# Storing the tail chunk of an attention-and-FFN kernel in halves of 64 rows

## The chip, the core and the metric

The kernel runs on one core of a Trainium2 chip. The metric is the device time of one execution in microseconds (us); lower is better. A core has five engines with a queue of their own each: TensorE (PE, with its weight loads PEld), VectorE (DVE), ScalarE (ACT), GpSimd (POOL) and SyncE (SP). In this kernel SP does no arithmetic: it issues DMA transfers and waits on semaphores.

## The reference

The inputs q, k and v have the shape 8 batches x 8 heads x 576 positions x 64. An attention without a score matrix is followed by a gated feed-forward network without a nonlinearity:

```
q_s = softmax(q, over the 64 features)
k_s = softmax(k, over the 576 positions)
kv  = einsum('bhsd,bhse->bhde', k_s, v)
x   = einsum('bhsd,bhde->bhse', q_s, kv)      -> 4608 tokens x 512
out = ((x @ w1) * (x @ w2)) @ w3 @ w_out      (w1, w2: 512 x 1024; w3: 1024 x 1024; w_out: 1024 x 512)
```

The output is 4608 x 512 in float32.

## The kernel before

Everything is multiplied in float16 and summed in float32. The product of w3 and w_out is made once at the start (`W3O`), so that a chunk needs two products of the first kind (`up`, with w1 and w2), one elementwise product (`ab`) and one product of the second kind (`down`, with `W3O`).

A batch has 576 tokens, nine for each of 64 rows (`HALF` = 64, `NJ` = 9: token = 9 * row + j). The main chunks, c = 0 to 7, take j = 0 to 7 of batch c, 512 tokens. What is left, j = 8 (`NM`) of all eight batches, is collected in `xtail` and makes a ninth chunk of 512 tokens, c = 8: the tail chunk. It runs last. Each chunk's second product goes over four blocks of 128 tokens (`tb` = 0 to 3) into the PSUM tile `po`; ACT or DVE copies a block to the SBUF tile `osb` (four buffers), and SP stores it.

- In a main chunk (`down`, `os`, `store`, the last at L824 to L829) a block holds two values of j, 64 rows each, so it is stored by two DMAs of 64 rows by 512 columns. Their rows lie nine rows of the output apart.
- In the tail chunk (`down2`, `os2`, `tail`, the last at L808 to L811) a block's 128 rows also lie nine rows of the output apart, and one DMA stores all of them. The fourth block is computed, copied and stored in two pieces of 256 columns (`c0`, `c1`), so there are five pieces: blocks 0, 1 and 2 whole, and then block 3's left and right part. In the names of the steps they are `8.0`, `8.1`, `8.2`, `8.3.0` and `8.3`.

The order of all steps on all engines is written out by hand in `ORDER`; a step is emitted where it stands there, and `PICKS` says which engine copies. The end of it is

```
down.8.0 os.7.3 st.7.3 down.8.1 os.8.0 st.8.0 down.8.2 os.8.1
st.8.1 down.8.3.0 os.8.2 st.8.2 down.8.3 os.8.3.0 st.8.3.0 os.8.3 st.8.3
```

where `st` is a store, so SP issues each store after the copy that it needs and before the next. The copies of blocks 0, 1, 2 and of the right part of block 3 are ACT's, that of the left part is DVE's.

Semaphores are given by the framework. The DMAs that SP issues take eight semaphores (0 to 7) in turn, and a DMA waits until the last one on the same semaphore has landed. When all is issued, SP waits for what is outstanding and closes the program (L915): nine wait instructions, the first for older semaphores of POOL's DMAs alone, the next eight for SP's DMA semaphores 0 to 7 in that order, most of them with another semaphore beside; then a drain, a barrier over all engines, and the clearing of the semaphores.

Of the kernel before, what the change touches and what calls it, by code (L numbers as in the profile page):

```python
# [229 lines left out]
def kernel(  # L230
# [11 lines left out]
    nc = tc.nc  # L242
    B, H, S, D = q.shape
    T, C = out.shape
    Fd = moe_w1.shape[1]
    P = 128
# [4 lines left out]
    HALF = P // G  # L251
    HH = H // G
    NHP = HH // 2
    NJ = S // HALF
    NM = 512 // HALF
# [32 lines left out]
    st = {}  # L288
# [476 lines left out]
    def chunk(c):  # L765
# [40 lines left out]
            copy(eng, st["osb", c, tb], st["po", c, tb])  # L806

        def tail(tb, c0, c1):  # L808
            nc.sync.dma_start(
                out=out.rearrange("(r j) c -> r j c", j=NJ)[tb * P:(tb + 1) * P, NM, c0:c1],  # L810
                in_=st["osb", c, tb, c0])  # L811

        def down2(tb, c0, c1):
            st["po", c, tb, c0] = p_o()
# [5 lines left out]
        def os2(tb, c0, c1, eng):  # L820
            st["osb", c, tb, c0] = work.tile([P, c1 - c0], F32, tag="osb", name="osb", bufs=4)
            copy(eng, st["osb", c, tb, c0], st["po", c, tb, c0][:, 0:c1 - c0])
# [29 lines left out]
        for sub in range(nf):  # L852
            for tb in range(4):
                if not SUBS[c][sub][0] <= tb * P < SUBS[c][sub][1]:
                    continue
                first = tb * P == SUBS[c][sub][0]
                needs = (([("ab", c, sub, u) for u in range(nu - 1)] + [("W3O", ft) for ft in range(N_FT)]
                          if first else []) + ([("down", c, tb - 1)] if tb else []))
                late = [("ab", c, sub, nu - 1)] if first else []
                if c < B:  # L860
                    A(("down", c, tb), "PE", 1.75, lambda tb=tb: down(tb), needs, takes="po", after=late)
                    A(("os", c, tb), moves(C), 0, lambda eng, tb=tb: os(tb, eng), [("down", c, tb)],
                      lead=EVICT, gives=[("down", c, tb)], takes="osb")
                    A(("st", c, tb), "SP", 1.15, lambda tb=tb: store(tb), [("os", c, tb)], lead=1e3,
                      gives=[("os", c, tb)], size=P * C * 4)
                    continue
                cuts = [0, C // 2, C] if tb == 3 else [0, C]
                for c0, c1 in zip(cuts, cuts[1:]):
                    it = (c, tb, c0) if c1 < C else (c, tb)
                    A(("down", *it), "PE", 0.02 + 1.73 * (c1 - c0) / C,  # L870
                      lambda tb=tb, c0=c0, c1=c1: down2(tb, c0, c1), needs, takes="po", after=late)
                    A(("os", *it), moves(c1 - c0), 0,
                      lambda eng, tb=tb, c0=c0, c1=c1: os2(tb, c0, c1, eng), [("down", *it)],
                      lead=EVICT, gives=[("down", *it)], takes="osb")
                    A(("st", *it), "SP", 0.57, lambda tb=tb, c0=c0, c1=c1: tail(tb, c0, c1),
                      [("os", *it)], lead=1e3, gives=[("os", *it)], size=P * (c1 - c0) * 4)
                    needs, late = needs + [("down", *it)], []
# [42 lines left out]
```

## Time and profile before

| | |
|---|---|
| median of three runs | 240.99 us (240.94 to 241.41) |
| the profiled execution | 240.52 us |
| its span, first to last instruction | 238.4 us |
| granted TensorE clock | 1.000 |
| PE busy | 230.7 us, 97% of the span |
| DVE, ACT, POOL busy | 180.0, 120.7 and 112.8 us |
| DMA | 45.66 MB, 192 GB/s on the mean |
| stores of the main chunks (L827) | 64, each 128 KB |
| stores of the tail chunk (L809) | 3 of 256 KB, 2 of 128 KB |

The span counts from the first to the last instruction; the profiled execution's own time has 2.1 us more around it. All times in the views are from the start of the span. A line of the timeline shows the start, the duration, the engine, the line of the kernel and the operation; "SPq" is SP's queue, and the duration of a DMA there is how long SP is busy issuing it, not how long the data take. The time from the start of the issue until the semaphore has its full count is called landing. In the views of one line, three numbers with slashes are the least, the median and the greatest duration in ns.

### The profile page before, as it was taken

What the parts mean: (1) busy time and instruction counts of PE and PEld (TensorE: products, weight loads), DVE (VectorE), ACT (ScalarE), POOL (GpSimd) and SP (SyncE); (2) the same over time, 40 slices, a digit from 0 to 9 for tenths busy, and PEclk for the clock granted to TensorE, in tenths of its full rate; (3) what the DMA queues carried; (4) which work ended last, traced back from release to release, by engine and by line L of the source; (5) the groups of instructions that cost most, each with busy time, mean ns of one, the idle gap of its engine ahead of it and who ended that gap; (6) DMA issues with size and microseconds to landing.
All of it is one profiled execution on the core that took longest, in us unless ns stands there. A gap on an engine that the chain in (4) does not pass through costs nothing.

```text
span 238.4 us, 4957 instructions
## 1 busy us (share of the span) xinstructions
PE 230.7 (97%) x1981; PEld 121.1 (51%) x1981; DVE 180.0 (76%) x275; ACT 120.7 (51%) x221; POOL 112.8 (47%) x74
## 2 busy tenths in 40 slices
PE   7899899999999999999999999999999999999994
PEld 2445559865857544444444444444454444444442
DVE  2977998898899989998998899787567444355610
ACT  1436764668768958768824683557323002200021
POOL 8345445479957986997662933328530000000000
PEclk9999999999999999999999999999999999999999
DMA  6999999999989999688988932540077231030143
GB/s 209 215 294 223 322 220 301 261 370 392 389 210 291 403 205 294 243 235 203 327 270 200 306 147 46 77 111 0 0 150 173 62 71 45 0 91 0 44 132 132
DMA packets 37894, 45.66 MB, mean 192 GB/s; under 512 B 15984, under 2 KB 22384, under 8 KB 37872
## 3 DMA queue, kind: packets, MB, share of 16 engines
q1 hardware_dynamic: 30080, 34.22, 49.3%
q0 software_dynamic: 7792, 11.14, 21.3%
q8 instruction: 15, 0.25, 0.4%
q14 instruction: 7, 0.06, 0.1%
HBM read 38.80 MB, written 9.44 MB: 202 GB/s over the span
## 4 chain that ended last, share of the span: by engine, by line
PE 86%; DMA 5%; DVE 3%; POOL 2%; issue 1%; ACT 1%; POOLq 0%; ACTq 0%
PE pab L779 52%; PE po L801 23%; DMA wosb<-in_moe_w_out_dram 5%; PE po L816 3%; PE pkv L544 2%; PE po L452 2%; PE xm L662 1%; DVE k L519 1%; POOL en L614 1%; POOL w L402 1%; PE po L662 1%; DVE kmx L493 1%; ACT ek L527 0%; PE pkv L554 0%; PE qtp L629 0%
## 5 line engine op out<-in xcount | busy, mean ns | idle before, releaser
L779 PE MATMUL pab<-x,w2sb 128*128 128x512 f16 (+1 forms) x320 | 66.0, 337 | 0.1
L779 PE MATMUL pab<-x,w1sb 128*128 128x512 f16 (+1 forms) x320 | 65.9, 336 | 0.0
L794 DVE TENSOR_TENSOR ab<-pab,bsb 128x512 f16<-128x512 f32 x72 | 48.9, 681 | 16.7 <-PE pab L779 15.2
L801 PE MATMUL po<-W3O,ab 128*128 128x512 f16 x256 | 59.5, 379 | 0.0
L779 PEld LDWEIGHTS <-w1sb 128*128 128x128 f16 x352 | 34.4, 98 | 27.9
L779 PEld LDWEIGHTS <-w2sb 128*128 128x128 f16 x352 | 33.4, 98 | 27.0 <-issue 0.7
L323 ACT CAST bsb<-pab 128x512 f16<-128x512 f32 x49 | 28.3, 585 | 36.5 <-PE pab L779 36.2
L801 PEld LDWEIGHTS <-ab 128*128 128x128 f16 x256 | 24.6, 98 | 28.8 <-issue 0.4
L519 POOL TENSOR_TENSOR k<-k,cb 128x1152 f32<-128x1152 f32 x13 | 33.9, 2626 | 8.1 <-DVE km L496 3.5
L582 POOL TENSOR_TENSOR q<-q,qm 128x1280 f32<-128x1280 f32 (+1 forms) x13 | 27.8, 2142 | 20.7 <-DVE qm L577 12.9
L614 POOL TENSOR_TENSOR en<-eq,qr 128x1024 f16<-128x1024 f16 (+1 forms) x14 | 29.2, 2093 | 17.4 <-DVE qr L607 8.0
L323 ACT COPY osb<-po 128x512 f32<-128x512 f32 (+1 forms) x26 | 14.9, 576 | 35.8 <-PE po L801 28.9
L577 DVE TENSOR_REDUCE qm<-q 128x16 f32<-128x1024 f32 (+1 forms) x16 | 21.4, 1340 | 3.5 <-DMA q<-in_q_dram 3.5
L323 DVE COPY osb<-po 128x512 f32<-128x512 f32 (+1 forms) x11 | 7.3, 667 | 20.8 <-PE po L801 13.7
L595 DVE TENSOR_REDUCE qr<-eq 128x16 f32<-128x1024 f16 (+1 forms) x16 | 21.3, 1341 | 0.5 <-ACT eq L590 0.5
L590 ACT ACTIVATE eq<-q 128x1024 f16<-128x1024 f32 (+1 forms) x16 | 18.6, 1163 | 5.6 <-DVE q L582 3.0
L527 ACT ACTIVATE ek<-k 128x1152 f16<-128x1152 f32 x16 | 18.6, 1165 | 3.6 <-POOL k L519 2.4
L323 DVE CAST bsb<-pab 128x512 f16<-128x512 f32 x23 | 15.8, 687 | 2.7 <-PE pab L779 2.2
L484 DVE TENSOR_REDUCE km<-k 128x128 f32<-128x1152 f32 x8 | 16.9, 2138 | 0.0
L452 PE MATMUL po<-wosb,w3T 128*128 128x512 f16 x64 | 15.0, 379 | 0.6 <-DMA wosb<-in_moe_w_out_dram 0.5
L327 ACT ACTIVATE x<-xm 128x512 f16<-128x512 f32 x14 | 7.9, 596 | 5.5 <-PE xm L662 5.4
L350 PE MATMUL po<-zero 128*128 128x512 f16 x25 | 8.4, 509 | 1.6 <-DVE zero L345 1.6
(70 smaller groups left out, 197.9 us busy)
## 6 DMA issues: line engine op xcount, KB each, us to landing
out_dram<-osb SPq DMA_DIRECT2D x66, 128.0 KB, 2.4
q<-in_q_dram SPq DMA_DIRECT2D x6, 1152.0 KB, 6.8
v<-in_v_dram SPq DMA_DIRECT2D x6, 1152.0 KB, 8.5
k<-in_k_dram SPq DMA_DIRECT2D x5, 1152.0 KB, 7.0
k<-in_k_dram POOLq DMA_DIRECT2D x3, 1152.0 KB, 14.6
v<-in_v_dram POOLq DMA_DIRECT2D x2, 576.0 KB, 14.4
w<-in_moe_w_dram POOLq DMA_DIRECT2D x2, 512.0 KB, 12.0
w<-in_moe_w_dram POOLq DMA_DIRECT2D x4, 256.0 KB, 14.0
```

Source lines behind the costliest of these rows:

```text
L323: return [(nc.scalar.copy if eng == "ACT" else engine[eng].tensor_copy)(out=out, in_=in_)]
L452: nc.tensor.matmul(st["pf", ft], lhsT=st["w3T", ft][:, gt, :], rhs=wosb[:, gt, :], start=(gt == 0), stop=(gt == N_FT - 1))
L519: return [engine[eng].tensor_tensor(out=kb[:, two(hp), :, :], in0=kb[:, two(hp), :, :], in1=st["cb", b][:, two(hp), None, :].broadcast_to( ...
L527: nc.scalar.activation(out=st["ek", b][:, hp, :, :].rearrange("p j (i d) -> p i j d", i=2), in_=kb[:, two(hp), :, :], func=AF.Exp)
L577: dve.tensor_reduce(out=st["qm", b][:, :, j], in_=qb[:, :, j, :], axis=AX.X, op=ALU.max)
L582: return [engine[eng].tensor_tensor(out=qb[:, :, j, :], in0=qb[:, :, j, :], in1=st["qm", b][:, :, j, None].broadcast_to([P, HH, n, D]), op ...
L590: nc.scalar.activation(out=st["eq", b, p], in_=qb[:, :, j, :], func=AF.Exp)
L595: dve.tensor_reduce(out=st["qr", b][:, :, slice(*PARTS[p])], in_=st["eq", b, p], axis=AX.X, op=ALU.add)
L614: return [engine[eng].tensor_tensor(out=st["en", b][:, j, :, :].rearrange("p j h d -> p h j d"), in0=st["eq", b, p], in1=st["qr", b][:, :, ...
L779: nc.tensor.matmul(st["p", one, c, sub, u][:, a * (t1 - t0):(a + 1) * (t1 - t0)], lhsT=w[:, ct, fb * P:(fb + 1) * P], rhs=x()[:, ct, t0:t1 ...
L794: dve.tensor_tensor(out=st["ab", c][:, nf * u:nf * u + nf, t0:t1], in0=cut(st["p", 0, c, sub, u]), in1=cut(st["bsb", c, sub, u]), op=ALU.mult)
L801: nc.tensor.matmul(st["po", c, tb], lhsT=st["ab", c][:, ft, tb * P:(tb + 1) * P], rhs=W3O[:, ft, :], start=(ft == 0), stop=(ft == N_FT - 1))
```

## The change

`tail` stores the first four of its five pieces in two DMAs of 64 rows each, one after the other, and the last piece, the right part of block 3, in one as before. So the tail chunk has nine stores instead of five: six of 64 rows x 512 columns, two of 64 x 256 and one of 128 x 256. The last transfer thereby takes the last of the eight semaphores. No other engine's instructions change, except that a copy that takes the buffer of a halved store now waits for two semaphores instead of one.

```
         def tail(tb, c0, c1):
-            nc.sync.dma_start(
-                out=out.rearrange("(r j) c -> r j c", j=NJ)[tb * P:(tb + 1) * P, NM, c0:c1],
-                in_=st["osb", c, tb, c0])
+            n = P if tb == 3 and c1 == C else HALF
+            for r in range(0, P, n):
+                nc.sync.dma_start(
+                    out=out.rearrange("(r j) c -> r j c", j=NJ)[tb * P + r:tb * P + r + n, NM, c0:c1],
+                    in_=st["osb", c, tb, c0][r:r + n, :])
```

The new lines shift the code behind them by two: L809 becomes L811, L827 becomes L829, and L915 becomes L917.

## The prediction

> **What bounds the kernel now.** I read the page first, then the end of the chain that ended last, then the order of time on ACT, DVE and SP's queue behind 228 us, and at last the waits of SP at the end of the program.
>
> ```profile
> span 238.4 us, 4957 instructions
> PE 230.7 (97%) x1981; PEld 121.1 (51%) x1981; DVE 180.0 (76%) x275; ACT 120.7 (51%) x221; POOL 112.8 (47%) x74
> ```
> ```profile
> 228.12 6.94 PE po L816 x40
> 235.06 0.03 ACTq L323
> 235.08 0.04 issue
> 235.12 0.37 ACT osb L323
> ```
> TensorE is busy 97% of the span, and the change does not touch it: the last matmuls end at 235.06, ACT copies the last half block out of PSUM by 235.49, and the span ends at 238.4. So some 2.9 us at the end belong to the last store and to closing the program. Only there, and in the 7 us before it in which the tail chunk is stored, can this change act.
>
> ```profile
> 229.92 0.59 ACT L323 COPY osb<-po 128x512 f32<-128x512 f32 x1 [1.19 <-PE po L816]
> 231.61 0.58 ACT L323 COPY osb<-po 128x512 f32<-128x512 f32 x1 [1.10 <-PE po L816]
> 233.33 0.58 ACT L323 COPY osb<-po 128x512 f32<-128x512 f32 x1 [1.14 <-PE po L816]
> 234.26 0.42 DVE L323 COPY osb<-po 128x256 f32<-128x256 f32 x1 [7.14 <-PE po L816]
> 235.12 0.37 ACT L323 COPY osb<-po 128x256 f32<-128x256 f32 x1 [1.21 <-PE po L816]
> ```
> ```profile
> 228.76 1.11 SPq L827 DMA_DIRECT2D out_dram<-osb  x2
> 230.53 0.38 SPq L809 DMA_DIRECT2D out_dram<-osb  x1
> 232.22 0.35 SPq L809 DMA_DIRECT2D out_dram<-osb  x1
> 233.94 0.33 SPq L809 DMA_DIRECT2D out_dram<-osb  x1
> 234.71 0.33 SPq L809 DMA_DIRECT2D out_dram<-osb  x1
> 235.52 0.33 SPq L809 DMA_DIRECT2D out_dram<-osb  x1
> ```
> Each store of the tail chunk (L809) is issued 0.02 to 0.03 us after the copy before it has ended: 229.92 + 0.59 = 230.51 and issue at 230.53, and so on to 235.49 and 235.52. SP's queue is idle in between; it waits for the copies, never they for it. What matters below is the distance from the third store to the last: 235.52 - 233.94 = 1.58 us, in which SP today issues two stores of 0.33 us.
>
> ```profile
> SPq L915 <- DMA out_dram<-osb: 1.1, 2, 0.7
> DMA to landing us min/median/max: 1.7/1.7/1.7
> L915 SPq EVENT_SEMAPHORE  x4: 28/28/28, 235.9 to 236.4; - x4
> L915 SPq EVENT_SEMAPHORE  x5: 28/28/28, 237.2 to 237.5; - x5
> L915 SPq EVENT_SEMAPHORE  x1: 28/28/28, 237.2 to 237.2; - x1
> L915 SPq EVENT_SEMAPHORE  x1: 28/28/28, 237.5 to 237.5; - x1
> L915 SPq DRAIN  x1: 7/7/7, 237.5 to 237.5; - x1
> ```
> These are the landing time of the last store alone, and SP's waits behind it. SP goes through nine waits: one for older semaphores of POOL's queue, then its own eight, 0 to 7, in that order. It stands still twice, 0.7 us at most, for stores. The last store lands at 235.52 + 1.7 = 237.2; the wait for its semaphore, number 3, passes, and four more come, though nothing is outstanding on them. Asked for in windows of 0.01 us, the first of the five appears in 237.23 to 237.24 (the first x1 row), the last in 237.47 to 237.48 (the second), and the drain in 237.53 to 237.54. So four waits by (237.47 - 237.23) / 4 = 0.06 us, **0.24 us**, lie between the last landing and the close.
>
> **The change, part by part.** The eight semaphores are taken in turn by SP's transfers. The tail's five stores now signal 7, 0, 1, 2, 3; with nine they signal 7, 0, 1, 2, 3, 4, 5, 6, 7. The last one then has the last wait of the list. The other eight waits, 8 x 0.06 = 0.48 us, are done while the last store is under way (1.7 us). That removes the four waits: **-0.24 us**. Cover: if an earlier half landed after the last store, up to one wait, 0.06 us, would come back.
>
> It adds four issues on SP. The trace of before has no halved store of the tail, but it has that form: the main chunks store each block as two DMAs of 64 rows by 512 columns, to rows of the output of the same spacing (L827).
>
> ```profile
> L827 SPq DMA_DIRECT2D out_dram<-osb x18: 466/531/597, 187.3 to 229.3; - x18
> DMA to landing us min/median/max: 2.2/2.3/2.4
> 174.54 2.46 SPq L827 DMA_DIRECT2D out_dram<-osb  x4
> L827 SPq DMA_DIRECT2D out_dram<-osb x4: 537/570/592, 174.5 to 176.4; - x4
> L827 SPq DMA_DIRECT2D out_dram<-osb x1: 466/466/466, 228.8 to 228.8; - x1
> L827 SPq DMA_DIRECT2D out_dram<-osb x1: 596/596/596, 229.3 to 229.3; - x1
> L809 SPq DMA_DIRECT2D out_dram<-osb x5: 332/332/382, 230.5 to 235.5; - x5
> ```
> A half is not cheaper to issue than a whole block; it is dearer. From 186 us on, nine pairs lie alone on SP's queue: the first of a pair takes 0.47 us, the second 0.60, against 0.33 to 0.38 for 128 rows. The last pair holds the queue 1.11 us, so 0.05 lie between its two issues (1.11 - 0.47 - 0.60, rounded up). Two pairs back to back (174.54) take 2.46 us; their four issues sum to 4 x 0.567 = 2.27 by the row's four values taken as 537, twice 570 and 592, which leaves 0.19: 0.05 in each pair and 0.09 between them, where a new pair also waits for a copy.
>
> Stepping through the changed tail with the copies where they are:
> - Block 0: issues from 230.53 to 230.53 + 1.11 = 231.64; block 1's copy ends at 232.19. Covered, by 0.55 us.
> - Block 1: 232.22 to 233.33; block 2's copy ends at 233.91. Covered, by 0.58 us.
> - Block 2: starts at 233.94 and would end at 235.05. DVE's copy of the first half of block 3 ends at 234.68. Not covered: that store, now the third issue in a row, starts at 235.05 + 0.09 = 235.14 instead of 234.71.
> - Block 3, first half: with block 2 it makes four 64-row issues back to back, 2.46 us less 0.07 for the first, which here finds the queue idle (0.47 in place of 0.54): to 233.94 + 2.39 = 236.33. They carry 256 columns instead of 512, but the L809 rows show 0.33 us for both widths, so I take no discount.
> - Last store: queued behind that, it starts at 236.33 + 0.09 = 236.42 instead of 235.52: **+0.90 us**. Its data have been ready since 235.49.
>
> Its own issue is of 128 rows, 0.33 us when alone. No 128-row store follows another closely at SP's pace; the second of a pair takes 0.13 us more than the first.
>
> ```profile
> L402 SPq DMA_DIRECT2D q<-in_q_dram x1: 374/374/374, 98.7 to 98.7; - x1
> L402 SPq DMA_DIRECT2D v<-in_v_dram x1: 593/593/593, 116.0 to 116.0; - x1
> ```
> A load of 128 partitions takes 0.37 us alone and 0.59 behind two pairs of stores, 0.22 more. So the bounds are 0 and 0.22, and a gain is excluded, since a queue that was just busy made nothing in these rows quicker. I take the pair's **+0.13 us**.
>
> Who else waits? Nothing stands behind the halves on SP but the last store and the close. ACT's last copy takes the buffer of block 0; the second half of that store lands at 231.04 + 2.4 = 233.4, 1.7 us before the copy at 235.12. Covered, and so is its one extra semaphore, in the 1.21 us for which ACT is idle. The second half of block 3a starts at 235.73 and lands by 2.4 at 238.1; the last store lands at 236.42 + 1.7 + 0.13 = 238.25, so it is still the last.
>
> Then the transfers themselves.
>
> ```profile
> 229.88:231.30 1.42, 1.42 (x8) 0.68 (x7) 0.00 (x0) 0.59 (x1) 0.00 (x0) 1.00 0.80 185
> 231.40:232.24 0.84, 0.84 (x5) 0.39 (x4) 0.00 (x0) 0.58 (x1) 0.00 (x0) 1.00 0.82 312
> ```
> The windows run from first to last packet of the last pair of halves and of the first whole store; the last column is GB/s. The same 256 KB take 1.42 us in halves and 0.84 whole. In blocks 0 to 2 nobody waits for that; for the last store it is a rival below. The Trainium skill (DMA: Bandwidth & Descriptors, Rules for kernel authors) says that two transfers to disjoint partition halves are not worth making, since both spread over all 16 DMA engines and serialize, and wants one transfer of 128 partitions. By that rule the halves gain nothing as transfers, and the trace goes further: at 185 against 312 GB/s they lose.
>
> Sum: -0.24 + 0.90 + 0.13 = **+0.79 us**. The profiled execution took 240.52 us, its span 238.4 and 2.1 around it; the sum makes it 241.31, with a span of 239.2. The median of the three runs, 240.99, lies 0.47 above the profiled one and is the base of the forecast: 240.99 + 0.79 = 241.78, or 241.8. A measurement of this kernel can tell about 0.2% from no change, 0.48 us.
>
> **Rivals.**
> - The halves issue as quickly as the tail's whole stores (not slower). If 64 rows of the tail cost 0.33 us as L809's 128 rows do, the four issues and their gaps take 1.32 + 0.19, and with 0.09 the last store starts at 235.54, 0.02 late: -0.22 us, 240.8. It decides at an issue of (1.58 + 0.24 - 0.28) / 4 = 0.385 us: below that the change gains. For it speaks that all five L809 issues are at or under 0.382; against it that all 18 quiet L827 issues are at or over 0.466, and that rows, not the place in the program, are what differs. The Trainium skill has a rule on this side: in DMA: Bandwidth & Descriptors, Issuing engines are not separate DMA queues, the time to initiate a DMA is called usually small beside the DMA. The trace agrees only in part: 0.47 to 0.60 us beside 2.2 to 2.4 to landing, but not small beside the slack of 1.58. Chance 0.06.
> - No queueing surcharge: each half at 0.47 because 1 KB rows or an idle chip's end make the second as quick as the first. The last store starts at 233.94 + 1.88 + 0.28 = 236.10: +0.58 - 0.24 = +0.34, 241.3. Within 0.2%. Against it: the surcharge is in the last pairs too, where DMA is all but idle. Chance 0.12.
> - The last store's data queue behind the halves'. The last pair's packets begin 1.12 us after its issue and go on for 1.42; from 235.14 that would be 237.68, if half the bytes took as long. The last store's packets would by the sum begin near 237.3, so up to 0.4 more: +1.2, 242.2. For it speaks the 185 GB/s; against it that 128 KB should need about half the time. Chance 0.10.
> - The change doesn't do what it says: the count of nine from semaphore 7 leaves no room for that.
>
> **How the numbers follow.** The forecast has 0.69. With the third rival, slower has 0.79. The first two make same, 0.18. Faster by over 0.2% has no mechanism, since the waits hold only 0.24 us; 0.03 is for what I have not seen. The range reaches from just under the second rival to just over the third, 241.2 to 242.3; the bounds of the last issue (0 and 0.22) and 0.2 us of scatter lie within it. It leaves out the first rival and odd runs.
>
> **What would show it.** Right: nine L811 issues, six of 64x512 with 0.47 and 0.60 in turn, the third pair running into the fourth; the last issue near 236.4; after the landing near 238.25 one wait and no four, then the drain. Step by step: the four waits are wrong if more than 0.1 us lies between landing and drain; the issues are wrong if a half takes under 0.4 us; the cover is wrong if block 0's or 1's second half delays the next pair. The whole is wrong if the last issue starts before 235.8: then the time is at or below 240.99.

## The result and the profile after

| | before | after |
|---|---|---|
| median of 14 runs each | 241.05 us | 241.65 us |
| ratio, with its 95% interval | | 1.0023 (1.0014 to 1.0031) |
| the profiled execution | 240.52 us | 241.78 us |
| its span | 238.4 us | 239.9 us |

The change makes the kernel slower, by 0.34 to 0.75 us over the interval, 0.55 in the middle. Here and below two executions that took far longer, one of the kernel before (302.79 us) and one of the kernel with eight more DMAs (612.54 us), are left out.

The page of after, its span and busy times, and the end of its chain:

```profile
span 239.9 us, 4962 instructions
...
PE 230.7 (96%) x1981; PEld 120.9 (50%) x1981; DVE 179.9 (75%) x275; ACT 120.7 (50%) x221; POOL 112.8 (47%) x74
```
```profile
228.73 6.94 PE po L818 x40
235.67 0.03 ACTq L323
235.69 0.04 issue
235.73 0.37 ACT osb L323
```
TensorE does the same work. The last 40 matmuls begin 0.61 us later in this execution than in the one before (228.73 against 228.12). That distance is there long before the tail (the 200th of the 1981 matmuls starts at 29.14 us in one trace and 29.75 in the other), where both kernels do the same. It is scatter: in the traces of the experiments below the same matmul starts anywhere from 28.98 to 29.90 us. So the two traces are compared from the tail's copies on, not from the start.

The timeline of after, ACT, DVE and SP's queue:

```profile
230.53 0.58 ACT L323 COPY osb<-po 128x512 f32<-128x512 f32 x1 [1.19 <-PE po L818]
232.22 0.59 ACT L323 COPY osb<-po 128x512 f32<-128x512 f32 x1 [1.10 <-PE po L818]
233.94 0.58 ACT L323 COPY osb<-po 128x512 f32<-128x512 f32 x1 [1.14 <-PE po L818]
234.87 0.42 DVE L323 COPY osb<-po 128x256 f32<-128x256 f32 x1 [7.14 <-PE po L818]
235.73 0.37 ACT L323 COPY osb<-po 128x256 f32<-128x256 f32 x1 [1.21 <-PE po L818]
```
```profile
231.15 1.10 SPq L811 DMA_DIRECT2D out_dram<-osb  x2
232.83 1.10 SPq L811 DMA_DIRECT2D out_dram<-osb  x2
234.56 1.11 SPq L811 DMA_DIRECT2D out_dram<-osb  x2
235.76 0.54 SPq L811 DMA_DIRECT2D out_dram<-osb  x1
236.34 0.59 SPq L811 DMA_DIRECT2D out_dram<-osb  x1
237.04 0.53 SPq L811 DMA_DIRECT2D out_dram<-osb  x1
```
Blocks 0 and 1: the pairs end at 232.25 and 233.93, before the next copies end at 232.81 and 234.52. Block 2's pair ends at 235.67, while DVE's copy has been ready since 235.29; five issues follow one another from 234.56 to 237.57. The last store's data are ready at 235.73 + 0.37 = 236.10; it is issued at 237.04, 0.94 us later, against 0.03 before.

The last store's landing, and SP's last wait and drain:

```profile
L811 SPq DMA_DIRECT2D out_dram<-osb x1: 533/533/533, 237.0 to 237.0; - x1
...
DMA to landing us min/median/max: 1.9/1.9/1.9
```
```profile
L917 SPq EVENT_SEMAPHORE  x1: 28/28/28, 239.0 to 239.0; - x1
L917 SPq DRAIN  x1: 13/13/13, 239.0 to 239.0; - x1
```
The last store lands at 238.95. The wait for it starts at 238.96, the drain at 239.03: 0.08 us from landing to drain where it was 0.32. The four waits are gone.

Below, "the stretch" is the time from the end of the last copy to the end of the span: 238.4 - 235.49 = 2.9 us before, 239.9 - 236.10 = 3.8 after (2.88 and 3.77, each read to 0.01 in the trace).

### The profile page after: what moved, and what is told of

Read it like the earlier page. It is cut to its first block, busy times and chain, and to the rows that moved or that the text cites. A ratio compares the mean times of both kernels' runs of the same rounds, so it can differ in the third digit from the quotient of the medians.

```text
span 239.9 us, 4962 instructions
## 1 busy us (share of the span) xinstructions
PE 230.7 (96%) x1981; PEld 120.9 (50%) x1981; DVE 179.9 (75%) x275; ACT 120.7 (50%) x221; POOL 112.8 (47%) x74
## 4 chain that ended last, share of the span: by engine, by line
PE 86%; DMA 7%; POOL 2%; DVE 1%; issue 1%; ACT 1%; ACTq 0%; DVEq 0%; POOLq 0%
PE pab L779 52%; PE po L801 23%; DMA w<-in_moe_w_dram 7%; PE po L818 3%; PE pkv L544 2%; PE po L452 2%; PE xm L662 1%; DVE k L519 1%; POOL w L402 1%; PE po L662 1%; PE w3t L440 0%; ACT ek L527 0%; PE pkv L554 0%; PE qtp L629 0%; POOL wosb L402 0%
## 5 line engine op out<-in xcount | busy, mean ns | idle before, releaser
L452 PEld LDWEIGHTS <-w3T 128*128 128x128 f16 x64 | 5.9, 98 | 8.0 <-issue 1.5
```

What stands on the lines that cost most here:

```text
L452: nc.tensor.matmul(st["pf", ft], lhsT=st["w3T", ft][:, gt, :], rhs=wosb[:, gt, :], start=(gt == 0), stop=(gt == N_FT - 1))
```

## The experiments

Except in the last three, the edits are in `tail` and `store`. Those of "halves without the turn" and of the two kernels behind it start from the changed kernel, the others from the kernel before. "The turn" is which of the eight semaphores the last store gets, and block 6.2 is block 2 of chunk 6. "Outside" is a run's time less its span, the mean over the runs of that kernel; spans are recorded to 0.1 us, so a single value is uncertain by 0.05. Over the runs taken beside the experiments the kernel before has 2.10 to 2.12 us outside, never under 2.06 nor over 2.18; after has 1.91, from 1.87 to 1.97.

**The turn of the semaphores alone.**

```
 def store(tb):
     for i in range(2):
         ...
+        n = HALF // 2 if (c, tb) in [(6, 2), (6, 3)] else HALF
+        for r in range(0, HALF, n):   # a DMA for each n rows
```


> The tail's five stores stay whole; two main-chunk blocks (6.2 and 6.3, after which SP's queue is idle for over 10 us) are stored in four DMAs of 32 rows instead of two of 64, so that the last store takes semaphore 7. Theory A (the turn of semaphores is worth the four waits, the halves cost through SP's queue): 0.24 us faster than before, ratio 0.9990, and about 0.08 us instead of 0.32 from the last landing to the drain. Rival B (the waits on idle semaphores are worth nothing at the end, because the closing barrier waits for something else): ratio 1.0000.

Measured: 240.49 us, ratio 0.9970 (0.9959 to 0.9981), faster by more than both theories said. Timeline, and the last wait and drain:

```profile
235.88 0.37 ACT L323 COPY osb<-po 128x256 f32<-128x256 f32 x1 [1.20 <-PE po L816]
...
236.28 0.33 SPq L809 DMA_DIRECT2D out_dram<-osb  x1
```
```profile
L917 SPq EVENT_SEMAPHORE  x1: 28/28/28, 238.0 to 238.0; - x1
L917 SPq DRAIN  x1: 13/13/13, 238.1 to 238.1; - x1
```
The last store is issued on time (236.25, 236.28), and 0.08 us lie between its landing and the drain. The stretch is 2.65 us, 0.23 less than before: that is theory A's gain. Rival B falls. But the measured gain is 0.72 us (0.46 to 0.99). Outside the span there are 1.78 us instead of 2.12, and with these 0.34 the parts make 0.57, which the interval holds. Neither theory had that.

**The halves without the turn.** Both edits, that of `store` and the change's, so that the last store is on semaphore 3 again.

> The tail in halves as in the changed kernel, and blocks 6.2 and 6.3 in four DMAs each as well, so that the last store is back on semaphore 3. Theory A: the changed kernel's cost without its gain: 0.24 us slower than the changed kernel, about +0.79 us over before, ratio 1.0033. Rival B: as the changed kernel, +0.55 us, 1.0023.

Measured: 241.73 us, 1.0024 (1.0014 to 1.0035). In time alone this doesn't part the theories. The trace does:

```profile
235.19 0.37 ACT L323 COPY osb<-po 128x256 f32<-128x256 f32 x1 [1.21 <-PE po L818]
...
236.49 0.53 SPq L811 DMA_DIRECT2D out_dram<-osb  x1
```
The last store is 0.93 us behind its copy, lands 1.91 us later, and 0.32 us, the wait for it and four more, lie between landing (238.40) and drain (238.73):

```profile
L919 SPq EVENT_SEMAPHORE  x5: 28/28/28, 238.4 to 238.7; - x5
L919 SPq DRAIN  x1: 7/7/7, 238.7 to 238.7; - x1
```
The stretch is 3.99 us, 0.22 more than in the changed kernel: the gain of the turn is there also behind halves. The time outside is 1.83 us.

**Halves only where they are covered.**

```
-            n = P if tb == 3 and c1 == C else HALF
+            n = HALF if tb < 2 else P
```
with block 6.2 in four DMAs.

> Only blocks 0 and 1 of the tail in halves, block 2 and both parts of block 3 whole; block 6.2 in four DMAs, so that the last store takes semaphore 7. Theory A: both pairs are done before the next copy is, so the last store is issued on time and only the gain is left: -0.24 us, 0.9990, as with the turn alone. Rival C (a half costs wherever it stands, through slower transfers or through copies that wait for two semaphores): about half of the halves' cost, +0.15 us or more, 1.0006 and up.

Measured: 240.47 us, 0.9975 (0.9966 to 0.9984); stretch 2.63 us.

```profile
235.85 0.37 ACT L323 COPY osb<-po 128x256 f32<-128x256 f32 x1 [1.21 <-PE po L818]
...
236.25 0.33 SPq L811 DMA_DIRECT2D out_dram<-osb  x1
```
On time, as with the turn alone: the halves of blocks 0 and 1 cost nothing. Outside 1.78 us.

**Halves only where they are not covered.**

```
-            n = P if tb == 3 and c1 == C else HALF
+            n = HALF if tb == 2 or c1 < C and tb == 3 else P
```
with block 6.2 in four DMAs.

> Only block 2 and the left part of block 3 in halves, blocks 0 and 1 whole; block 6.2 in four DMAs, last store on semaphore 7. Theory A: the whole cost of the changed kernel, the last store issued 0.9 us after its copy ends: +0.55 to +0.8 us, ratio 1.0023 to 1.0033. Rival C: about half the cost, with the gain +0.15 us, 1.0006.

Measured: 241.69 us, 1.0024 (1.0014 to 1.0034), stretch 3.76 us.

```profile
235.51 0.37 ACT L323 COPY osb<-po 128x256 f32<-128x256 f32 x1 [1.21 <-PE po L818]
...
236.82 0.54 SPq L811 DMA_DIRECT2D out_dram<-osb  x1
```
0.94 us late, the whole of the changed kernel's cost (stretch 3.77). Rival C falls; the cost sits in the four halves of block 2 and of the left part of block 3.

**Cut by columns instead of rows.**

```
+            m = c1 if tb == 3 and c1 == C else (c0 + c1) // 2
+            for a, e in ([(c0, m), (m, c1)] if m < c1 else [(c0, c1)]):
                 # ... the DMA as before, of 128 rows and columns a to e
```


> The same first four pieces of the tail in two DMAs each, but cut by columns: 128 rows x 256 (and 128 x 128 for the left part of block 3); nine stores, the last on semaphore 7. Theory A (each issue holds SP's queue, more so behind another issue): 0.33 us for an issue that finds the queue idle and 0.53 behind another, as the changed kernel's last store showed, put the last store 0.62 us late; with 0.2 for its own issue and 0.24 gained, the stretch from the last copy to the end of the span grows by about 0.6 us. Rival E (only 64-row stores are dear to issue; 128 rows take 0.33 us also behind another): last store 0.02 us late, the stretch shrinks by 0.22 us. Rival F (what cost was the slow transfer of 64 rows, not the issue): the last store is issued late as in the changed kernel but lands 1.7 us later instead of 1.9.

Measured: 241.01 us, 0.9998 (0.9989 to 1.0008).

```profile
L811 SPq DMA_DIRECT2D out_dram<-osb x9: 332/390/449, 231.0 to 236.3; - x9
...
DMA to landing us min/median/max: 1.6/1.7/1.8
```
```profile
235.64 0.37 ACT L323 COPY osb<-po 128x256 f32<-128x256 f32 x1 [1.21 <-PE po L818]
...
236.35 0.38 SPq L811 DMA_DIRECT2D out_dram<-osb  x1
```
No version of the issue's price was right: 128 rows take 0.33 to 0.38 us on an idle queue and 0.38 to 0.45 behind another issue, between rival E's 0.33 and theory A's 0.53. So the last store is 0.34 us late, between 0.02 and 0.62, and the stretch is 2.99 us, 0.11 over before. As many DMAs, the same bytes and the same turn cost 0.78 us less in the stretch than with 64 rows each (2.99 against 3.77). Rival F, slow transfers with the last store issued as late as in the changed kernel, falls: it is issued earlier. The 0.11 us are more than given back outside the span (1.91 us, 0.20 less), and the interval holds the sum of the two, -0.09.

**Two and eight more DMAs, tail whole.** The edit of `store` for block 6.2 alone, and for blocks 6.0, 6.2, 6.3 and 7.1.

> All tail stores whole, only block 6.2 in four DMAs: two more DMAs than before, last store on semaphore 5. Theory A: two idle waits are left, 0.12 us, so 0.20 us from the last landing to the drain and the span 0.12 us shorter. The time outside the span was 2.12 us before, and 1.78 to 1.92 in every kernel with four or eight more DMAs on SP. Theory N (it goes with the number of DMAs or instructions, not with the turn): near 1.95 us, between them. Rival P (any difference of the program changes it): 1.8 us.

> All tail stores whole, blocks 6.0, 6.2, 6.3 and 7.1 in four DMAs each: eight more DMAs than before, last store back on semaphore 3. Theory A: 0.32 us from the last landing to the drain, the span as before (239.0 us on the median). Outside the span: theory N 1.8 us, so 240.75 us and ratio 0.9987 without any gain from the turn; if instead the whole of 0.6 us came from the turn, 241.1 us, ratio 1.0000.

Measured: with two more 240.67 us, 0.9985 (0.9977 to 0.9994), 0.20 us from landing (237.08) to drain on semaphore 5, with the wait for the last store and two more, and 1.91 us outside. With eight more 241.00 us, 0.9998 (0.9989 to 1.0006), span 239.0 on the median, and 1.98 us outside, the mean of ten runs that lie from 1.81 to 2.09 (the profiled execution is the one of 612.54 us, so no view of it is shown). The view with two more:

```profile
L917 SPq EVENT_SEMAPHORE  x3: 28/28/28, 237.1 to 237.2; - x3
L917 SPq DRAIN  x1: 13/13/13, 237.3 to 237.3; - x1
```
The turn's part is as theory A has it: 0.32, 0.20 and 0.08 us with the last store on 3, 5 and 7. The time outside goes with neither theory: two more DMAs have 1.91, four more 1.78 or 1.91, eight more 1.83 or 1.98. Sorted by the number of ACT's instructions in the compiled program, however, it falls into place; the next three kernels test that. (The traces show two fewer in each kernel, 311 before and 312 after, with the same differences. In the trace of after the added one is a wait in front of ACT's last copy, for the second half of block 0.)

**Only ACT's number of instructions.**

```
         def os(tb, eng):
             ...
+            if (c, tb) == (6, 2):
+                for _ in range(n):                       # n = 1 or 2; spare is a new tile
+                    nc.scalar.copy(out=spare, in_=epst)  # 128 x 1
```


> The kernel before with one more instruction on ACT: a copy of 128 x 1 into a spare tile behind the copy step of block 6.2, where ACT is idle; stores, semaphores and all else as before. Over the kernels run so far the time outside the span goes by the number of ACT's instructions in the program: 313 (before) 2.12 us, 314 (the changed kernel, late halves, column halves, two more DMAs) 1.91, 315 (turn only, early halves) 1.78, 316 1.83, 317 1.98. Theory Q (it is that number): 314 here, so 1.91 us, the span as before, 0.2 us faster, ratio 0.9991. Rival R (it is the DMAs or the turn, and ACT's number only goes along with them through the copies' waits): 2.12 us, ratio 1.0000.

> As the one before, with two such copies: 315 instructions on ACT. Theory Q: 1.78 us outside the span, 0.33 us faster than before, ratio 0.9986. Rival R: 2.12 us, ratio 1.0000.

> The changed kernel with one such copy on ACT: 315 instructions on ACT instead of 314. Theory Q: 1.78 us outside the span instead of 1.91, so 241.5 us, ratio to before 1.0018. Rival R: 1.91 us, ratio 1.0023.

| | ACT's instructions | outside, expected by Q | measured (least to most) | median | ratio |
|---|---|---|---|---|---|
| before + 1 | 314 | 1.91 us | 1.90 (1.87 to 1.95) | 240.77 us | 0.9992 (0.9983 to 1.0001) |
| before + 2 | 315 | 1.78 | 1.78 (1.74 to 1.82) | 240.76 | 0.9987 (0.9978 to 0.9995) |
| changed kernel + 1 | 315 | 1.78 | 1.78 (1.73 to 1.83) | 241.51 | 1.0020 (1.0011 to 1.0030) |

Theory Q holds to 0.01 us, with no store touched in two of the three. Rival R falls. The ratios agree, though that of one copy doesn't exclude 1. What in ACT's program makes this time is not known from these runs. The waits in front of ACT's copies before and after, and the spare copy in the kernel before with one:

```profile
L323 ACTq EVENT_SEMAPHORE  x68: 17/17/5323, 11.1 to 233.3; - x68
...
L323 ACTq EVENT_SEMAPHORE  x69: 17/17/5325, 11.0 to 234.1; - x69
...
L810 ACT COPY spare<-epst x1: 195/195/195, 195.5 to 195.5; 128x1 f32<-128x1 f32 x1
```
The stretch is 2.89, 2.87 and 3.75 us in these three and 2.78 with two more DMAs. For each kernel whose stretch is given, the changed one included, the change of the stretch and that of the time outside add up to a value within the measured interval.

**A version that beats both** is one of these: the turn alone, 240.49 us, 0.9970 of before. By the trace 0.23 us of it come from the waits; by the runs 0.34 come from outside the span, where ACT happens to have 315 instructions. Halves of blocks 0 and 1 besides (240.47) add nothing to that.

## Why the prediction was right, and where it was off

The forecast was 241.8 us (241.2 to 242.3), +0.79; measured were 241.65, and +0.55 by the ratio. Direction and mechanism were right. By its steps:

- **The four waits, -0.24.** 0.32 us from landing to drain became 0.08. Shown three ways: gone alone, back with the halves on semaphore 3, half gone on semaphore 5.
- **The last store's late issue, +0.90.** 0.94 us behind its copy instead of 0.03, +0.91. The L827 rows gave each price: the third and fourth issue in a row took 0.54 and 0.59 us, 1.13 together, where the prediction's sum leaves 1.14; and 1 KB rows gave no discount. The cover of blocks 0 and 1 held with 0.56 and 0.59 us to spare (0.55 and 0.58 in the prediction), and leaving them whole changes nothing.
- **The last store's own issue, +0.13.** Mis-sized: 0.53 us instead of 0.33 is +0.20, and it landed 1.91 instead of 1.69 us after its start, +0.22. The nearest row was not the second of a pair but the load behind two pairs (+0.22), which stood as the upper bound.
- **The queue of data.** It added nothing. 1.9 - 0.53 = 1.4 us from the end of the issue to landing is what 1.7 - 0.33 was before. That rival is out for the last store. The halves are slow all the same. By the Trainium skill's rule that the prediction weighed (DMA: Bandwidth & Descriptors, Rules for kernel authors), two transfers to disjoint partition halves serialize and are not worth making. The trace agrees that they are not, and the rate is lower besides: the packets of after's block 0 run in the window below, at 186 GB/s, against 312 for the whole store before. In the traces a packet of 2 KB takes 0.147 us there in the median and 0.086 in the whole store; why is open.

```profile
232.27:233.67 1.40, 1.40 (x8) 0.65 (x7) 0.00 (x0) 0.53 (x1) 0.00 (x0) 1.00 0.81 186
```
- **What lies around the span, "2.1 us".** This is the step that failed. It was carried over as a constant, and it was 1.91 us: -0.20. The prediction even named the cause in passing, one extra semaphore for ACT's last copy, and costed it at nothing, since ACT is idle there. In the span it does cost nothing. But the second semaphore is one more wait instruction on ACT (69 in front of its copies instead of 68), 314 instructions instead of 313, and with one spare copy in its place the kernel before has 1.90.

Together: -0.24 + 0.91 + 0.22 - 0.20 = +0.69 us, which lies in the measured interval, 0.34 to 0.75; +0.79 lies just above it. That the forecast came so near is in part luck: the last issue was priced 0.09 too low and the time around the span 0.20 too high, and these errors go opposite ways. The rival in which halves issue as fast as whole blocks is out by the rows themselves (0.47 to 0.60 us each), and so is that without a surcharge. The time from landing to drain, the last issue, the covered pairs and the copies' order all showed what the prediction had asked of them.

## What to carry to other kernels

Near the end of a program, price a split transfer by what its issues hold of the queue, and by the slack between the last copies, not by its bytes: here four issues of 64 rows took 2.4 us where 1.58 were free. Closing waits are worth a look, but they come cheaper by shifting the turn where the queue is idle. Where a few tenths of a microsecond matter, compare time less span as well as span, since one or two more instructions on ACT moved the difference by 0.2 to 0.3 us here.

## What was unexpected of the hardware

- The issue of a store holds SP's queue longer for 64 rows than for 32 or 128. In the traces of all kernels here but the one with eight more DMAs, from 186 us on, an issue on an idle queue took 0.47 to 0.49 us for 64 rows, 0.32 to 0.39 for 32 and 0.33 to 0.38 for 128; behind an issue of the same kind it took 0.54 to 0.61, 0.41 to 0.43 and 0.38 to 0.45. A 128-row store behind a 64-row pair took 0.53 to 0.54. Why is open. The rows for 32, from the kernel with the turn alone (the first of four, then another four in a row):

```profile
L829 SPq DMA_DIRECT2D out_dram<-osb x1: 321/321/321, 211.4 to 211.4; - x1
...
L829 SPq DMA_DIRECT2D out_dram<-osb x4: 387/416/428, 197.7 to 199.0; - x4
```
- The time outside the span went by the number of ACT's instructions and not evenly: 2.1 us at 313, 1.91 at 314 (five kernels) and 1.78 at 315 (four), with every run within 0.08 of its kernel's mean. At 316 and 317 there is one kernel each, with 1.83 and 1.98, and at 317 the runs spread from 1.81 to 2.09. Why is open.
